# Loading q and k of two batches four heads at a time, in a Nystrom attention with two MLPs

## The chip, the cores and the metric

One core of a Trainium2 chip runs the whole program. The metric is device time in microseconds (us) of one execution. The engines are PE (TensorE, matrix products), DVE (VectorE), ACT (ScalarE), POOL (GpSimd) and SP (SyncE, which here only issues DMAs). "PEld" is the loading of a matmul's stationary operand, which runs beside the matmuls. Data moves on 16 DMA engines that all queues share.

## The reference

Attention with landmarks, then two MLPs on its output. q, k and v have 4 batches, 8 heads, 576 tokens and 64 columns per head.

```
q_lm = q.reshape(B, H, 32, 18, D).mean(axis=3)      # 32 landmarks, each the mean of 18 tokens
k_lm = k.reshape(B, H, 32, 18, D).mean(axis=3)
A  = softmax(scale * q    @ k_lm.T)
Bm = softmax(scale * q_lm @ k_lm.T)
C  = softmax(scale * q_lm @ k.T)
Z  = Bm.T / (norms of Bm); six times: Z = 2*Z - Z @ Bm @ Z
x  = A @ Z @ C @ v                                  # per head, then heads side by side: 2304 x 512
x  = (silu(rms_norm(x) @ w_gate) * (rms_norm(x) @ w_val)) @ w_out      # hidden width 1536
y  = (s * relu(x @ w_in)**2 + b) @ w_out2                              # hidden width 2048
```

The weights come in as 64-bit floats and are narrowed to 32 bits on the core. All large products are made in three passes of halves (a high and a low part of each operand).

## The kernel before

**A planner orders the work.** Each piece of work is handed to a list scheduler with the engines that may do it, an estimated duration and a key (class `Scheduler`, L87). Before anything is issued, it plays the whole program through with its own estimates and so fixes the order of the instructions on every engine. On the chip every engine then works through its own list strictly in order; an instruction that waits holds up all that stand behind it on its engine. Where the planner expects PE to be idle in the first stretch, it puts in matmuls that nobody reads (`warm`, L1245, line 1248 in the profile). What the planner thinks of a load's cost is the number in the load's entry (5.2 for one q or k tile on SP, 9.5 for v).

**Attention** (L401) is done batch by batch. A tile of q or k has 128 partitions: four heads, 32 landmark segments each; a partition holds 18 tokens of 64 columns, 1152 floats. There are two tiles of each, g = 0 and 1, with the heads 2h + g for h = 0 to 3. `load_heads` (L444, DMAs at L446) fills a tile by four DMAs, one head to 32 partitions each. In batch 0 the q tiles are issued on ACT's queue, all others on SP's. v (L457, DMAs at L460) comes in by 18 DMAs of 64 KB per batch. The later batches reuse the same tiles, so their loads wait until the batch before has been read.

Then come the segment sums (`seg_sum`, L471; on DVE at L474 in batch 0, on POOL at L488 to L493 later), their transposes into landmark tiles (L498, L501), the transposes of q and k (`transposed`, L519, PE at L528, copied out by ACT at L532), and the score matmuls, one 32 x 288 block for each head and half (`scores`, L642, L660). In batches 0 and 1 (`fine` false) a score matmul reads the 32 landmark columns of its head and the 32 partitions' columns of its head's transposed tile; in batches 2 and 3 the scores are made with whole tiles in three passes (L648) from a DVE transpose (L537). `c_side` (L669) does C and C @ v, `a_side` (L740) does A and its transpose back; L872 scales A with the norm; `gw` (L810) is the last product of Z, C and v that the first MLP needs.

**The first MLP** runs in units, one for each batch and each 128 columns of the hidden width (12 units a batch): `fused` (L984, PE at L993) folds `gw` into the gate and value weights, `first_mm` (L1009, PE at L1016) multiplies with A, L1032 to L1038 make silu times value, and `out_mm` (L1045, PE at L1061 and L1065) multiplies with w_out. The attention of batch b + 1 runs between the units of batch b.

**Weights** are narrowed by `narrow` (L897): a 512 KB load into one of three `stage` buffers (L904, L906), two ACT instructions (L917, L919), two DVE instructions (L921, L924). The 36 narrowed tiles of the first MLP are stored back (`keptg`, `kepto`) and read again for batches 1 to 3. Below, S1, S2, ... are the stage loads and N1, N2, ... the narrowings, in order; S(n+3) needs the buffer that N(n) has read.

**The second MLP** (L1081, L969: lines 975 and 1091) takes the rest of the run.

**Semaphores of the DMAs.** All DMAs of SP and ACT share eight semaphores in turn (DMAHW0 to 7 in the rows below): a DMA whose semaphore is still in use waits on its engine's list until the eighth DMA before it has landed.

Of the kernel before, what the change touches and what calls it, by code (L numbers as in the profile page):

```python
# [35 lines left out]
SCORE = 0.56  # L36
# [213 lines left out]
def tile_nystrom_attention_two_mlps(  # L250
# [16 lines left out]
    B, H, S, D = q.shape  # L267
    NT, DM = out.shape
    M = 32
    SEG = S // M  # L270
    HB = SEG // 2
    HC = HB * M
# [96 lines left out]
    def consts(_):  # L369
# [12 lines left out]
        out=ident, in_=ones, pattern=[[-1, 128]], compare_op=ALU.is_equal,  # L382
# [18 lines left out]
    def attention(b, t0, t1):  # L401
        first = b == 0
        slow = COLD if first else 1.0
        fine = b >= FINE
# [5 lines left out]
        def at(alts, pos, fn, r=(), w=(), pair=False):  # L410
            mine.append(op(alts, 0.0, fn, r, w, pair or set(alts) == {"dve", "pool"}))
            mine[-1].spare = {"dve": SPA if b else SPA0}
            if not first and "sp" not in mine[-1].alts:
                mine[-1].after = RELB
            at_ops.append(mine[-1])
# [24 lines left out]
        for nm, a in (("k", k), ("q", q)):  # L440
            for g in range(2):
                t = src[nm, g] = Buf(qk_r[nm, g])

                def load_heads(e, t=t, a=a, g=g):  # L444
                    for h in range(4):
                        e.dma_start(  # L446
                            out=t.t[32 * h:32 * h + 32].rearrange("p (t d) -> p t d", d=D),
                            in_=a[b, 2 * h + g].rearrange("(i t) d -> i t d", t=SEG))

                at(("act" if first and nm == "q" else "sp", 2.2 if first and nm == "q" else 5.2),  # L450
                   -0.3 if b else 0, load_heads, w=[t])
        vs = Buf(v_r)

        def vt():
# [5 lines left out]
                e.dma_start(out=vt()[32 * (n % 4):32 * (n % 4) + 32, n // 4], in_=sv[token(b, n)])  # L460

        at(("sp", 9.5), -0.25 if b else 0.01, load_v, w=[vs])

        lmT, bd, tt = {}, {}, {}
        for i, (nm, g) in enumerate((("k", 0), ("k", 1), ("q", 0), ("q", 1))):
# [19 lines left out]
            else:  # L485
# [4 lines left out]
                for n in (4, 2, 1):  # L490
# [3 lines left out]
                    out=lm.t, in0=y()[:, 0], in1=y()[:, 8], op=ALU.add), r=[tmp], w=[lm])  # L494
# [56 lines left out]
        def b_mm(_):  # L551
            for g in range(2):
                if not fine:
                    for h in range(4):
                        p = slice(32 * h, 32 * h + 32)
                        nc.tensor.matmul(
                            out=pB.t[p, 32 * g:32 * g + 32], lhsT=bd["q", g].t[0:D, p],
                            rhs=bd["k", g].t[0:D, p], start=True, stop=True)
                    continue
                for e in range(2):  # L560
                    nc.tensor.matmul(
                        out=pB.t[:, 32 * g:32 * g + 32], lhsT=bdv(bd["q", g])[:, e],
                        rhs=lmT["k", g].t[:, 32 * e:32 * e + 32], start=(e == 0), stop=(e == 1))
# [76 lines left out]
                    else e.tensor_copy(out=zy(1), in_=v2(pY2))), r=[pY2], w=[ZY])  # L640

        def scores(ps, nm, g, hf, p0, r, w):  # L642
            d, t = bd["kq"[nm == "k"], g], tt[nm, g]
            if fine:
                def mm(_):
                    for e in range(2):
# [8 lines left out]
                return  # L655
            def mm(_):
                for h in range(4):
                    p = slice(32 * h, 32 * h + 32)
                    e = slice(D * hf, D * hf + D)
                    nc.tensor.matmul(  # L660
                        out=ps.t[p, 0:HC], lhsT=d.t[e, p],
                        rhs=t.t[e].rearrange("p (t m) -> p t m", m=128)[:, :, p], start=True, stop=True)

            at(("pe", SCORE), p0 + 0.02, mm, r=[d, *[(t, i) for i in range(3)], *r], w=[ps, *w])


        Cv = Buf(cv_r)

        def c_side(g, p0):  # L669
            transposed("k", g, p0)  # L670
            pC = [Buf(ps_r), Buf(ps_r)]
            eC = Buf(eC0_r if first else eC_r)
            cm, cs, rc = Buf(sm_r), Buf(sm_r), Buf(sm_r)
# [65 lines left out]

        def a_side(hf, g, p0):  # L740
            if hf == 0:
                transposed("q", g, p0)
            pA, A, a = Buf(ps_r), Buf(a_ring), Buf(AT_r)
            am, asum = Buf(sm_r), Buf(sm_r)
            AT[hf, g] = a
# [438 lines left out]
    for n in range(len(units) + HALF + 1):  # L1184
        t = T[n]
# [99 lines left out]
```

## Time and profile before

| | us |
|---|---|
| median of three timed runs | 906.83 (901.38 to 908.39) |
| the profiled execution's own time | 903.9 |
| its span, first to last instruction | 902.2 |
| PE busy | 870.2 (96%) |
| DVE busy | 700.9 (78%) |
| ACT busy | 430.0 (48%) |
| mean share of the 16 DMA engines in q1, SP's queue | 38.3% |

The span falls into three stretches. Up to about 61 us the attention of batch 0 runs, and PE is filled up with matmuls of line 1248. From there to about 162 us the first MLP's units of batch 0 run beside the attention of batch 1 and the narrowing of the weights. After that PE works nearly without a gap to the end. PE's busy share therefore says little of the first two stretches: there it counts the filler too.

### The profile page before, as it was taken

The page shows a single profiled execution, that of the slowest core. Times are in us where ns is not written, and L with a number is a line of the kernel's source. Part 1 is how long each engine was busy: PE and PEld are TensorE (multiplying, and loading weights), DVE is VectorE, ACT ScalarE, POOL GpSimd, SP SyncE. Part 2 cuts the span into 40 slices and gives each one's busy share as a digit, 9 for nine tenths or more (in the row PEclk, how much of TensorE's full clock was granted, in tenths as well). Part 3 has the DMA queues.
Part 4 walks back from the last instruction along what each step waited for, and adds up shares of the span by engine and source line. Part 5 has one row for each costly group of instructions (what it writes and reads, how often), then busy time and mean ns, then how long its engine had stood idle before and what let it go on. Part 6 is the DMA issues. An engine that isn't in the chain of part 4 may idle for free.

```text
span 902.2 us, 17055 instructions
## 1 busy us (share of the span) xinstructions
PE 870.2 (96%) x6453; PEld 726.4 (81%) x6453; DVE 700.9 (78%) x1486; ACT 430.0 (48%) x902; POOL 114.4 (13%) x152
## 2 busy tenths in 40 slices
PE   8897899899999999999999999999999999999997
PEld 5576666798788898899888988888888888888896
DVE  5768889889888889799889866676667666666686
ACT  3565566535465345555656533343343334333453
POOL 0442034500465004300000000000000000000000
PEclk9898999999999999999999999999999999999999
DMA  7778998886444432348887200010001000100100
GB/s 162 198 214 283 247 280 236 271 241 216 119 144 141 143 116 84 106 146 272 286 262 252 56 1 1 0 47 1 1 1 47 1 1 1 47 1 1 27 22 24
DMA packets 72899, 105.99 MB, mean 117 GB/s; under 512 B 25968, under 2 KB 46448, under 8 KB 72816
## 3 DMA queue, kind: packets, MB, share of 16 engines
q1 hardware_dynamic: 72240, 103.45, 38.3%
q10 hardware_dynamic: 576, 1.44, 0.7%
q8 instruction: 51, 0.84, 0.4%
q14 instruction: 32, 0.26, 0.1%
HBM read 90.70 MB, written 14.16 MB: 116 GB/s over the span
## 4 chain that ended last, share of the span: by engine, by line
PE 83%; DVE 8%; DMA 5%; ACT 2%; issue 1%; SPq 1%; ACTq 0%; DVEq 0%
PE bank L975 22%; PE bank L1091 22%; PE bank L1016 15%; PE bank L1065 12%; PE bank L1061 3%; PE bank L993 3%; DMA region<-in_q_dram 2%; DVE cmag L921 2%; DMA stage<-in_moe_w_out_dram 2%; PE bank L648 1%; PE bank L828 1%; DMA stage<-in_moe_w_gate_dram 1%; PE bank L1248 1%; DVE wl L893 1%; DVE rawg L924 1%
## 5 line engine op out<-in xcount | busy, mean ns | idle before, releaser
L1016 PE MATMUL bank<-xh,uh 128*128 128x288 f32 x384 | 124.2, 323 | 6.4 <-DVE hbuf L1034 3.1
L975 PE MATMUL bank<-xh,ul 128*128 128x512 f32 (+1 forms) x320 | 117.7, 368 | 0.0
L975 PE MATMUL bank<-xh,uh 128*128 128x512 f32 (+1 forms) x320 | 117.6, 368 | 0.0
L975 PE MATMUL bank<-xl,uh 128*128 128x512 f32 (+1 forms) x320 | 117.6, 368 | 0.0
L1016 PE MATMUL bank<-xl,uh 128*128 128x288 f32 x384 | 114.8, 299 | 0.0
L1016 PE MATMUL bank<-xh,ul 128*128 128x288 f32 x384 | 114.7, 299 | 0.0
L1091 PE MATMUL bank<-wh,hh 128*128 128x512 f32 x288 | 112.4, 390 | 0.3 <-DVE hh L892 0.3
L1091 PE MATMUL bank<-wl,hh 128*128 128x512 f32 x288 | 112.3, 390 | 0.0
L1226 ACT ACTIVATE hbuf<-bank 128x512 f32<-128x512 f32 (+1 forms) x79 | 43.9, 556 | 143.4 <-PE bank L975 143.3
L1091 PE MATMUL bank<-wh,hl 128*128 128x512 f32 x288 | 112.0, 389 | 0.0
L1016 PEld LDWEIGHTS bank<-xh,uh 128*128 128x128 f32 x384 | 73.6, 192 | 27.3 <-issue 5.0
L1065 PE MATMUL bank<-hh,wh 128*128 128x288 f32 x288 | 87.9, 305 | 1.1 <-ACT xbuf L1075 1.1
L1065 PE MATMUL bank<-hl,wh 128*128 128x288 f32 x288 | 84.9, 295 | 0.1
L1065 PE MATMUL bank<-hh,wl 128*128 128x288 f32 x288 | 84.6, 294 | 0.0
L893 DVE TENSOR_TENSOR hl<-hbuf,hh 128x512 fp32r<-128x512 f32 (+2 forms) x123 | 73.1, 595 | 2.3
L1016 PEld LDWEIGHTS bank<-xl,uh 128*128 128x128 f32 x384 | 73.7, 192 | 0.5
L1016 PEld LDWEIGHTS bank<-xh,ul 128*128 128x128 f32 x384 | 73.7, 192 | 0.0
L975 PEld LDWEIGHTS bank<-xh,uh 128*128 128x128 f32 x320 | 60.2, 188 | 11.1
L975 PEld LDWEIGHTS bank<-xl,uh 128*128 128x128 f32 x320 | 60.0, 188 | 10.9
L975 PEld LDWEIGHTS bank<-xh,ul 128*128 128x128 f32 x320 | 60.1, 188 | 10.2
L917 ACT ACTIVATE ca<-stage 128x512 f32<-128x512 f32 x68 | 45.9, 675 | 42.6 <-DMA stage<-in_moe_w_out_dram 12.0
L892 DVE CAST uh<-region 128x512 fp32r<-128x512 f32 x56 | 23.9, 426 | 54.4 <-PE bank L975 54.4
(193 smaller groups left out, 1822.9 us busy)
## 6 DMA issues: line engine op xcount, KB each, us to landing
rawo<-kepto SPq DMA_DIRECT2D x84, 256.0 KB, 3.3
rawg<-keptg SPq DMA_DIRECT2D x36, 512.0 KB, 3.9
stage<-in_moe_w_out_dram SPq DMA_DIRECT2D x28, 512.0 KB, 5.2
stage<-in_moe_w_in_dram SPq DMA_DIRECT2D x16, 512.0 KB, 4.6
stage<-in_moe_w_gate_dram SPq DMA_DIRECT2D x12, 512.0 KB, 5.3
stage<-in_moe_w_val_dram SPq DMA_DIRECT2D x12, 512.0 KB, 5.5
keptg<-rawg SPq DMA_DIRECT2D x12, 512.0 KB, 6.3
region<-in_k_dram SPq DMA_DIRECT2D x32, 144.0 KB, 5.3
```

Of the source, the lines that this page charges most:

```text
L648: nc.tensor.matmul(out=ps.t[:, 0:HC], lhsT=part(u, "bd")[:, 128 * e:128 * e + 128], rhs=part(y, "t").rearrange("p (t e i) -> p t e i", e=2 ...
L892: else e.tensor_copy(out=hi(), in_=src())), r=r, w=[wh], pair=True)
L893: b = op({"dve": t_dve(n), "pool": t_pool(n)}, key, lambda e: e.tensor_tensor(out=lo(), in0=src(), in1=hi().bitcast(F32), op=ALU.subtract) ...
L917: op(("act", 0.08 + t_act(512)), key, lambda e: e.activation(out=a.t, in_=word(1).bitcast(F32), func=ACTF.Copy, scale=2.0 ** -112), r=[st, ...
L921: op(("dve", t_dve(512)), key, lambda e: e.scalar_tensor_tensor(out=m.t, in0=word(1), scalar=-2 ** 31, in1=m.t, op0=ALU.bitwise_and, op1=A ...
L975: nc.tensor.matmul(out=ps.t[:, 0:n], lhsT=w[a].t[:, ks], rhs=x[y].t[:, kd, 0:n], start=(kd == 0 and i == 0), stop=(kd == KD - 1 and i == 2))
L993: nc.tensor.matmul(out=pU[g].t[m, 0:256], lhsT=gw[b].t[p, m], rhs=r.t[p, :, 128 * k:128 * k + 128], start=True, stop=True)
L1016: nc.tensor.matmul(out=ps.t[:, 0:HC], lhsT=u[a].t[:, 256 * g + 128 * part:256 * g + 128 * part + 128], rhs=x[y].t.rearrange("p k n -> p (k ...
L1061: nc.tensor.matmul(out=A[c].t[:, 0:HC], lhsT=r.t[:, 128 * c:128 * c + 128], rhs=h.t, start=(f == 0), stop=(f == F1 - 1))
L1065: nc.tensor.matmul(out=A[c].t[:, 0:HC], lhsT=w[a].t[:, 128 * c:128 * c + 128], rhs=hs[y].t[:, 0:HC], start=(f == 0 and i == 0), stop=(f == ...
L1091: nc.tensor.matmul(out=A[c].t, lhsT=hs[a].t[:, s], rhs=w[y].t, start=(f == 0 and i == 0), stop=(f == F2 - 1 and i == 2))
L1226: e.activation(out=r.t[:, 0:n], in_=ps.t[:, 0:n], func=ACTF.Relu) if e is nc.scalar
```

## The change

Batches 0 and 1 load each q and k tile with a single DMA of four heads to 128 partitions; the tile then holds the heads 4i to 4i + 3 in order, not the heads of one parity. The sums, landmarks and transposes are the same per tile. The matmuls that combine heads (`b_mm`, `scores`) look up in which tile and which partitions head 2h + g now lies (`loaded`) and write where they wrote before. Since a group g now reads both tiles, `c_side(0)` transposes both k tiles, and `a_side` of g = 0 both q tiles. Batches 2 and 3 keep the four DMAs a tile. q of batch 0 is issued on SP's queue, and the planner's cost for a tile of batches 0 and 1 is 3.64 in place of 5.2 (and 2.2 for q on ACT). With other costs, the planner also orders other things anew.

```diff
                 def load_heads(e, t=t, a=a, g=g):
+                    if not fine:
+                        e.dma_start(
+                            out=t.t.rearrange("p (t d) -> p t d", d=D),
+                            in_=a[b, 4 * g:4 * g + 4].rearrange("h (i t) d -> (h i) t d", t=SEG))
+                        return
                     for h in range(4):
                         e.dma_start(
                             out=t.t[32 * h:32 * h + 32].rearrange("p (t d) -> p t d", d=D),
                             in_=a[b, 2 * h + g].rearrange("(i t) d -> i t d", t=SEG))
 
-                at(("act" if first and nm == "q" else "sp", 2.2 if first and nm == "q" else 5.2),
-                   -0.3 if b else 0, load_heads, w=[t])
+                at(("sp", 5.2 if fine else 3.64), -0.3 if b else 0, load_heads, w=[t])
...
+        def loaded(g, h):
+
+            n = 2 * h + g
+            return n // 4, slice(32 * (n % 4), 32 * (n % 4) + 32)
...
             def mm(_):
                 for h in range(4):
-                    p = slice(32 * h, 32 * h + 32)
+                    i, p = loaded(g, h)
                     e = slice(D * hf, D * hf + D)
                     nc.tensor.matmul(
-                        out=ps.t[p, 0:HC], lhsT=d.t[e, p],
-                        rhs=t.t[e].rearrange("p (t m) -> p t m", m=128)[:, :, p], start=True, stop=True)
-
-            at(("pe", SCORE), p0 + 0.02, mm, r=[d, *[(t, i) for i in range(3)], *r], w=[ps, *w])
+                        out=ps.t[32 * h:32 * h + 32, 0:HC], lhsT=bd[other, i].t[e, p],
+                        rhs=tt[nm, i].t[e].rearrange("p (t m) -> p t m", m=128)[:, :, p], start=True, stop=True)
+
+            at(("pe", SCORE), p0 + 0.02, mm, r=[*[bd[other, j] for j in range(2)],
+                *[(tt[nm, j], i) for j in range(2) for i in range(3)], *r], w=[ps, *w])
...
         def c_side(g, p0):
-            transposed("k", g, p0)
+            for j in (g,) if fine else (0, 1) if g == 0 else ():
+                transposed("k", j, p0)
...
             if hf == 0:
-                transposed("q", g, p0)
+                for j in (g,) if fine else (0, 1) if g == 0 else ():
+                    transposed("q", j, p0)
```

SP's list at its start, before, with the semaphores that each DMA waits for (`region` holds the q, k and v tiles):

```order
L446 DMA region<-in_k_dram 32x1152 x4
L446 DMA region<-in_k_dram 32x1152 [waits DMAHW1_49]
L446 DMA region<-in_k_dram 32x1152 [waits DMAHW3_49]
L446 DMA region<-in_k_dram 32x1152 [waits DMAHW5_49]
L446 DMA region<-in_k_dram 32x1152 [waits DMAHW7_49]
L460 DMA region<-in_v_dram 32x8x64 [waits DMAHW0_49]
L460 DMA region<-in_v_dram 32x8x64 [waits DMAHW1_49]
```

And now:

```order
L446 DMA region<-in_k_dram 128x1152 x2
L446 DMA region<-in_q_dram 128x1152 x2
L464 DMA region<-in_v_dram 32x8x64 x4
L464 DMA region<-in_v_dram 32x8x64 [waits DMAHW0_49]
L464 DMA region<-in_v_dram 32x8x64 [waits DMAHW1_49]
L464 DMA region<-in_v_dram 32x8x64 [waits DMAHW2_49]
L464 DMA region<-in_v_dram 32x8x64 [waits DMAHW3_49]
L464 DMA region<-in_v_dram 32x8x64 [waits DMAHW4_49]
```

Four DMAs stand where sixteen stood (eight of them on ACT's list). The fifth to eighth of v now wait for the four of k and q, and the ninth for the first of v.

SP's list around the loads of batch 1, before (the first row closes the small loads after S1 to S3; the `stage` rows are S4, S5, S6 and S7):

```order
L388 DMA b_sb<-in_moe_b_dram 128x1
L446 DMA region<-in_k_dram 32x1152 x8
L446 DMA region<-in_q_dram 32x1152 x8
L906 DMA stage_91<-in_moe_w_val_dram 128x4x128
L906 DMA stage_92<-in_moe_w_gate_dram 128x4x128
L906 DMA stage_93<-in_moe_w_val_dram 128x4x128
L937 DMA keptg_114<-rawg_85 128x1024
L460 DMA region<-in_v_dram 32x8x64 x18
L906 DMA stage_91<-in_moe_w_gate_dram 128x4x128
```

And now:

```order
L388 DMA b_sb<-in_moe_b_dram 128x1
L446 DMA region<-in_k_dram 128x1152 x2
L446 DMA region<-in_q_dram 128x1152 x2
L464 DMA region<-in_v_dram 32x8x64 x18
L919 DMA stage_91<-in_moe_w_val_dram 128x4x128
L919 DMA stage_92<-in_moe_w_gate_dram 128x4x128
L919 DMA stage_93<-in_moe_w_val_dram 128x4x128
L950 DMA keptg_114<-rawg_85 128x1024
L451 DMA region<-in_k_dram 32x1152 x4
L919 DMA stage_91<-in_moe_w_gate_dram 128x4x128
```

The 18 loads of v for batch 1 have moved from between S6 and S7 to ahead of S4. Four loads of k for batch 2 now stand ahead of S7.

SP's list around the loads of q and v for batch 2, before (the `stage` rows are S29 to S33):

```order
L906 DMA stage_92<-in_moe_w_val_dram 128x4x128
L446 DMA region<-in_q_dram 32x1152 x4
L904 DMA stage_93<-in_moe_w_out_dram 128x512
L949 DMA kepto_129<-rawo_90 128x512
L446 DMA region<-in_q_dram 32x1152 x4
L904 DMA stage_91<-in_moe_w_out_dram 128x512
L460 DMA region<-in_v_dram 32x8x64 x18
L906 DMA stage_92<-in_moe_w_gate_dram 128x4x128
L906 DMA stage_93<-in_moe_w_val_dram 128x4x128
```

And now:

```order
L919 DMA stage_92<-in_moe_w_val_dram 128x4x128
L451 DMA region<-in_q_dram 32x1152 x8
L917 DMA stage_93<-in_moe_w_out_dram 128x512
L962 DMA kepto_129<-rawo_90 128x512
L464 DMA region<-in_v_dram 32x8x64 x18
L917 DMA stage_91<-in_moe_w_out_dram 128x512
L919 DMA stage_92<-in_moe_w_gate_dram 128x4x128
L919 DMA stage_93<-in_moe_w_val_dram 128x4x128
```

S31 stood ahead of the 18 loads of v and now stands behind them; all eight loads of q stand ahead of S30.

The rest of the lists is ordered much as before. DVE has the same instructions ahead of the last two L872 of batch 1, but for two or three. PE has 121 filler matmuls in place of 161, the same matmuls otherwise, and in batch 1 the 18 transposes of q stand together between the ninth and the tenth group of L993, where nine of them stood between the eighth and the ninth. Ahead of the first two L866 of batch 0 (which broadcast the norm for L872) there were 35 and then 15 fillers on PE's list, and now there are none.

## Rows read from the trace of the kernel before

**Rows 1.** Windows: us; each engine's busy us (instructions); PE clock, DMA share, GB/s.

```profile
56.00:66.00 10.00, 9.99 (x91) 8.57 (x89) 4.98 (x13) 5.37 (x11) 6.49 (x10) 1.00 0.76 222
...
120.00:140.00 20.00, 19.07 (x282) 13.41 (x281) 18.39 (x51) 12.10 (x30) 10.27 (x14) 1.00 0.91 272
...
160.00:200.00 40.00, 39.00 (x312) 34.47 (x313) 34.36 (x72) 16.23 (x38) 12.63 (x17) 0.96 0.85 253
...
500.00:600.00 100.00, 100.00 (x472) 84.32 (x472) 72.73 (x132) 40.21 (x70) 0.00 (x0) 1.00 0.07 17
```

**Rows 2.** Chain that ended last, first 62 us: by line; two pieces (start, us).

```profile
by line: DMA region<-in_q_dram 19.2%; PE bank L1248 12.4%; SPq L460 9.6%; DMA stage<-in_moe_w_gate_dram 7.2%; PE bank L848 6.8%; issue 5.4%; DVE cmag L921 3.6%; PE bank L828 3.6%; PE bank L726 2.5%; DVE region L762 2.3%; ACTq L446 2.1%; DVE
...
8.89 5.23 DMA region<-in_q_dram
...
20.64 4.49 DMA stage<-in_moe_w_gate_dram
```

**Rows 3.** Timeline of the start: start us, us, engine, line; idle time before, its releaser.

```profile
0.80 8.41 ACTq L446 DMA_DIRECT2D region<-in_q_dram  x8
0.80 8.12 SPq L446 DMA_DIRECT2D region<-in_k_dram  x8
...
8.71 2.12 DVE L474 TENSOR_REDUCE region<-region 128x64 f32<-128x1152 f32 x1 [7.13 <-DMA region<-in_k_dram]
...
10.09 10.51 SPq L460 DMA_DIRECT2D region<-in_v_dram  x18
...
13.62 6.30 DVE L474 TENSOR_REDUCE region<-region 128x64 f32<-128x1152 f32 x3 [2.78 <-DMA region<-in_k_dram]
...
25.15 0.66 ACT L917 ACTIVATE ca<-stage 128x512 f32<-128x512 f32 x1 [2.57 <-DMA stage<-in_moe_w_gate_dram]
```

**Rows 4.** Windows of 2 us in the start, columns as in rows 1.

```profile
0.00:2.00 2.00, 0.88 (x5) 0.64 (x6) 0.53 (x17) 0.00 (x0) 0.50 (x5) 1.00 0.24 28
...
4.00:6.00 2.00, 2.00 (x13) 1.36 (x11) 0.00 (x0) 0.00 (x0) 0.00 (x0) 1.00 1.01 214
6.00:8.00 2.00, 0.11 (x2) 0.00 (x0) 0.00 (x0) 0.00 (x0) 0.00 (x0) 1.00 1.00 205
...
24.00:26.00 2.00, 0.33 (x16) 0.22 (x16) 1.83 (x11) 0.85 (x2) 0.00 (x0) 0.98 1.08 373
```

**Rows 5.** The page's DMA issues: count, KB each, median us to landing.

```profile
rawg<-keptg SPq DMA_DIRECT2D x36, 512.0 KB, 3.9
...
region<-in_k_dram SPq DMA_DIRECT2D x32, 144.0 KB, 5.3
```

**Rows 6.** Timeline of SP's queue around v of batches 1 and 2.

```profile
47.64 11.07 SPq L460 DMA_DIRECT2D region<-in_v_dram  x18
58.81 0.40 SPq L906 DMA_DIRECT2D stage<-in_moe_w_gate_dram  x1
...
127.26 1.85 SPq L446 DMA_DIRECT2D region<-in_q_dram  x4
...
135.94 0.35 SPq L904 DMA_DIRECT2D stage<-in_moe_w_out_dram  x1
136.39 11.83 SPq L460 DMA_DIRECT2D region<-in_v_dram  x18
```

**Rows 7.** Timeline of PE and DVE between 52 and 66 us.

```profile
52.84 4.16 PE L1248 MATMUL bank<-ones 128*128 128x256 bf16 x35
...
62.70 0.46 DVE L1034 SCALAR_TENSOR_TENSOR hbuf<-hbuf,bank 128x288 f32<-128x288 f32 x1 [2.23 <-ACT hbuf L1032]
...
65.89 1.22 DVE L921 SCALAR_TENSOR_TENSOR cmag<-stage,cmag 128x512 int32<-128x512 int32 x1
```

**Rows 8.** Timeline of DVE and PE towards the end of batch 1's attention.

```profile
116.96 0.66 PE L993 MATMUL bank<-rawg,gw 64*32 64x256 f32 x16
...
134.69 0.66 PE L993 MATMUL bank<-rawg,gw 64*32 64x256 f32 x16
...
146.05 0.69 DVE L921 SCALAR_TENSOR_TENSOR cmag<-stage,cmag 128x512 int32<-128x512 int32 x1
...
161.65 0.66 PE L993 MATMUL bank<-rawg,gw 64*32 64x256 f32 x16
```

More of the change, by code (lines that the diff above doesn't have):

```diff
@@ L554, in b_mm @@
                     for h in range(4):
-                        p = slice(32 * h, 32 * h + 32)
+                        i, p = loaded(g, h)
                         nc.tensor.matmul(
-                            out=pB.t[p, 32 * g:32 * g + 32], lhsT=bd["q", g].t[0:D, p],
-                            rhs=bd["k", g].t[0:D, p], start=True, stop=True)
+                            out=pB.t[32 * h:32 * h + 32, 32 * g:32 * g + 32], lhsT=bd["q", i].t[0:D, p],
+                            rhs=bd["k", i].t[0:D, p], start=True, stop=True)
                     continue
@@ L642, in scores @@
         def scores(ps, nm, g, hf, p0, r, w):
-            d, t = bd["kq"[nm == "k"], g], tt[nm, g]
+            other = "kq"[nm == "k"]
             if fine:
@@ L657, in mm @@
                 for h in range(4):
-                    p = slice(32 * h, 32 * h + 32)
+                    i, p = loaded(g, h)
                     e = slice(D * hf, D * hf + D)
                     nc.tensor.matmul(
-                        out=ps.t[p, 0:HC], lhsT=d.t[e, p],
-                        rhs=t.t[e].rearrange("p (t m) -> p t m", m=128)[:, :, p], start=True, stop=True)
-            at(("pe", SCORE), p0 + 0.02, mm, r=[d, *[(t, i) for i in range(3)], *r], w=[ps, *w])
+                        out=ps.t[32 * h:32 * h + 32, 0:HC], lhsT=bd[other, i].t[e, p],
+                        rhs=tt[nm, i].t[e].rearrange("p (t m) -> p t m", m=128)[:, :, p], start=True, stop=True)
+            at(("pe", SCORE), p0 + 0.02, mm, r=[*[bd[other, j] for j in range(2)],
+                *[(tt[nm, j], i) for j in range(2) for i in range(3)], *r], w=[ps, *w])
         Cv = Buf(cv_r)
         def c_side(g, p0):
-            transposed("k", g, p0)
+            for j in (g,) if fine else (0, 1) if g == 0 else ():
+                transposed("k", j, p0)
             pC = [Buf(ps_r), Buf(ps_r)]
```

## The prediction

> **What bounds the kernel now.** I read the windows first. From 160 us on PE is busy 39.0 of 40 us, later 100 of 100 [rows 1]: that stretch is PE's, the change takes no product out of it, and it will last as long as now, wherever it starts. So the question is how much earlier it starts. Between 120 and 140 us DVE is busy 18.4 of 20 us [rows 1]; it does batch 1's attention, the narrowing and the units' work, and its list sets the pace from about 66 us on. Between 56 and 66 us it is busy only 4.98 of 10 us [rows 1]: there it waits. The chain of the first 62 us [rows 2] names, as its largest part, the loads of q (19.2%), and then the issuing of v (9.6%) and the first stage load (7.2%). The timeline of the start [rows 3] says how: DVE's first segment sum starts at 8.71 us, when the first k tile has landed; it idles 2.78 us more for the second, and the last three sums end at 13.62 + 6.30 = 19.92. ACT idles 2.57 us until 25.15 for the first stage load, with the attention's work behind that instruction on its list.
>
> Why the loads take so long shows in the short windows [rows 4]. With all 16 DMA engines busy (share 1.00 and 1.01) they move 205 and 214 GB/s into tiles of 32 partitions; between 24 and 26 us, mostly stage loads to 128 partitions, 373 GB/s at a share of 1.08. The page agrees: 512 KB to 128 partitions land in 3.9 us, 144 KB to 32 partitions in 5.3 [rows 5].
>
> **The change, part by part.**
>
> *The first sums.* Batch 0's 16 loads are 16 x 144 KiB = 2.36 MB. The first 2 us move 28 GB/s, 56 KB [rows 4], so data flows from about 1.75 us; at 215 GB/s 2.36 MB take 11.0 us, to 12.75. The last load lands at 8.89 + 5.23 = 14.12 [rows 2], 1.4 us behind its last byte. At 373 GB/s a tile of 590 KB takes 1.6 us, and k comes first, no longer mixed with q: the tiles land at 1.75 + 1.6 + 1.4 = 4.75, then 6.3, 7.9 and 9.5 us. Four sums of 2.1 us (6.30/3) from 4.75 run without a gap to 13.15, against 19.92: **6.8 us** earlier. The lower bound is the old rate: tiles at 5.9, 8.6, 11.4 and 14.1 us, sums done at 16.2, 3.7 us earlier, since k still goes ahead of q. I take 373, because its row is the nearest to 128-partition loads with full engines.
>
> [...]
>
> *The stage loads.* SP issues v's 18 loads from 10.09 to 20.60 [rows 3], the later ones 0.49 us apart, because each waits for the eighth DMA before it. Now the fifth to eighth wait for the k and q tiles and the ninth for the first v load, behind the last q tile, about 10.0 us; ten more follow at 0.49 us, so S1 goes out at about 14.9 instead of 20.64, 5.7 us earlier. With the old rate it is 1.1. This does not add to the first term: the chain needs both. But ACT's wait of 2.57 us shrinks, as its list now has the softmax of C ahead of the first stage tile: 0 to 2.6, I take **1.0**.
>
> *The hole at 56 to 66 us.* S7 is issued at 58.81, after v of batch 1 has held SP for 11.07 us [rows 6], and N7 starts on DVE at 65.89 [rows 7]. Ahead of it DVE also waits for PE, where 35 fillers of 4.16 us in all stand before the L866 that DVE needs, and then 2.23 us for the first hidden tile [rows 7]. Now v stands ahead of S4, in time in which SP waits for a free stage buffer anyhow, and those fillers are gone. S7 needs N4, and k of batch 2 is ahead of it, so the hole does not close for certain. DVE's idle time there is 10 - 4.98 = 5.0 us: between 0 and 5.0, I take **3.0**.
>
> *S31.* It was issued at 135.94, just ahead of the 11.83 us of v for batch 2 [rows 6]; now it follows them. Its N31 runs at 146.05 [rows 8]. With a lead of 9 us over the old times SP reaches q at 118, and eight loads of 0.46 us (1.85/4), S30 and v take it to about 134.5. S31 then lands 4.5 us later (4.49 for the first stage load [rows 2]), and after 1.3 us of ACT N31 could start at 140.3, where DVE would be ready at 137. Some of these 3.3 us fill with other work that DVE has before N31: 0 to 3.3 lost, I take **2.5**.
>
> *At nothing:* the eight issues on ACT, which has nothing else before 9 us; the 40 fillers, which are not waited for where PE is the bound; batch 1's own faster loads, long landed before its work is due; the score matmuls, which are as many and as large as before.
>
> Sum: 6.8 + 1.0 + 3.0 - 2.5 = **8.3 us**. The profiled execution took 903.9 us, which gives 895.6. The median of the timed runs lies 2.9 above that execution; on it the sum gives 898.5. The mean of all four executions is 905.1, which gives 896.8: I say **897**.
>
> **The rivals.**
>
> *The transfer is no faster.* The DMA engines are already full at 205 GB/s [rows 4]; if they and not the target limit the rate, four DMAs in one save only waits. [...] Against it stand the 373 GB/s at the same share. The sums gain 3.7, S1 gains 1.1, and since the chain needs both, some 2 to 3 remain, and the hole gives 1: 901 to 902.
>
> *The lead is used up.* From 66 to 162 us DVE's list could be paced by something that does not move with the start: the three stage buffers, or the DMA engines, at a share of 0.91 [rows 1]. Then the units catch up with the old times: 903 to 905. Against it, both start earlier too, and the faster loads of two batches relieve the engines.
>
> *More.* The hole closes, S31 costs nothing, ACT's wait goes: 7.0 + 2.6 + 5.0 = 14.6, 889 to 892.
>
> *Slower: batch 1's q comes a unit late.* Its transposes need both transposed-tile buffers, which both groups of k now hold until all scores of C are made; so all 18 stand behind the ninth L993, where nine stood ahead of it. From the ninth L993, at 116.96, to the tenth are 17.7 us [rows 8]. If the work on A falls back by one such stretch, less the third of it that already lay there, some 12 us, the twelfth L993, at 161.65 us [rows 8], with which PE's own stretch begins, loses 12 and gains 8.3: 903.9 + 3.7 = 907.6, and with the smaller gain of the first rival 913. It decides from a delay of 8.3 us on. Against it, the scores of C on PE's list have moved forward in exchange.
>
> **How the numbers follow.** Chances: the forecast (a gain of 5 to 11 us) 0.50, no faster transfer 0.17, lead used up 0.12, more 0.15, slower 0.06. The runs shown lie up to 0.6% from their median, so about 1% is what can be told from no change. 1% is 9 us, and the forecast's own range lies about that line: half of it, most of "more" and a little of the rest count as faster, 0.45; slower by over 1% takes the last rival nearly whole, 0.05; the rest, 0.50, is within. The range is 889 to 905: the lower end is "more", the upper takes in the first two rivals; left out are the slower case and half of what lies at the ends, under 0.2.
>
> **What would show it.** Right: the first L474 near 4.8 us and the last ending near 13.2; windows above 330 GB/s before 10 us; S1 near 15 and S7 near 48 to 50 us; N7 before 58; the twelfth L993 near 153 us; from there an unchanged stretch. Wrong: about 215 GB/s in the first 10 us (first rival); N7 early but the twelfth L993 near 161 (second); more than 20 us from the ninth L993 to the tenth (slower). What would make it wrong without these is a new stall on PE's or DVE's list after 160 us, where DVE works 34.4 of 40 us [rows 1] and has little room.

## The result, and the profile after

The changed kernel takes **893.49 us** (median of four runs, 892.03 to 895.56) against 905.4 (four runs of the kernel before): ratio **0.9869, 95% interval 0.9838 to 0.9899**. Timed a second time, beside other kernels, it took 896.31 (six runs), ratio 0.9896 (0.9872 to 0.9921). Over all ten runs the median is 895.2, some 10 us less than before. The forecast was 897.0, range 889 to 905. The rows below are of the profiled run of 892.31 us, span 890.7.

The start, on DVE (start us, us, engine, line, operation; in brackets the idle time before and its releaser) and in windows of 2 us (columns as in rows 1):

```profile
4.47 8.32 DVE L484 TENSOR_REDUCE region<-region 128x64 f32<-128x1152 f32 x4 [2.89 <-DMA region<-in_k_dram]
```

```profile
2.00:4.00 2.00, 2.00 (x11) 1.40 (x10) 0.00 (x0) 0.08 (x1) 0.00 (x0) 1.00 0.98 325
4.00:6.00 2.00, 2.00 (x14) 1.61 (x12) 1.53 (x1) 0.53 (x2) 0.00 (x0) 1.00 1.00 396
6.00:8.00 2.00, 1.43 (x14) 1.16 (x14) 2.00 (x2) 1.39 (x4) 0.00 (x0) 1.00 1.03 405
```

L484 is the old L474. The sums no longer wait for single tiles: four in one piece, done at 12.79 where rows 3 have 19.92. At the same share of the DMA engines, 1.00, the loads now move 396 GB/s where they moved 214 [rows 4].

SP's queue up to the seventh stage load (S1 at 15.79, S4 at 37.79, S7 at 52.45), and the first stage tile's ACT instruction:

```profile
1.73 0.91 SPq L446 DMA_DIRECT2D region<-in_q_dram  x2
2.68 13.06 SPq L464 DMA_DIRECT2D region<-in_v_dram  x18
15.79 0.45 SPq L919 DMA_DIRECT2D stage<-in_moe_w_gate_dram  x1
...
20.39 1.48 SPq L446 DMA_DIRECT2D region<-in_q_dram  x2
27.74 9.94 SPq L464 DMA_DIRECT2D region<-in_v_dram  x18
37.79 0.39 SPq L919 DMA_DIRECT2D stage<-in_moe_w_val_dram  x1
...
50.62 1.73 SPq L451 DMA_DIRECT2D region<-in_k_dram  x4
52.45 0.38 SPq L919 DMA_DIRECT2D stage<-in_moe_w_gate_dram  x1
```

```profile
20.03 0.67 ACT L930 ACTIVATE ca<-stage 128x512 f32<-128x512 f32 x1 [0.37 <-DMA stage<-in_moe_w_gate_dram]
```

S1 is 4.85 us earlier than in rows 2, and ACT's wait for it fell from 2.57 us [rows 3] to 0.37. v of batch 1 is issued at 27.74 instead of 47.64 [rows 6], ahead of S4. S7 comes 6.4 us earlier than in rows 6, behind the k loads of batch 2, before which SP stands from 40.72 to 50.62.

On DVE, N6 and N7, and later N31 and N32; then the last two pairs of L885 (before: L872), by which attention ends:

```profile
55.73 0.68 DVE L934 SCALAR_TENSOR_TENSOR cmag<-stage,cmag 128x512 int32<-128x512 int32 x1
59.99 0.74 DVE L934 SCALAR_TENSOR_TENSOR cmag<-stage,cmag 128x512 int32<-128x512 int32 x1
...
141.60 0.69 DVE L934 SCALAR_TENSOR_TENSOR cmag<-stage,cmag 128x512 int32<-128x512 int32 x1 [1.70 <-ACT cmag L932]
143.73 0.69 DVE L934 SCALAR_TENSOR_TENSOR cmag<-stage,cmag 128x512 int32<-128x512 int32 x1
...
149.91 0.81 DVE L885 TENSOR_TENSOR region<-region,bank 128x288 f32<-128x288 f32 x2
151.63 0.82 DVE L885 TENSOR_TENSOR region<-region,bank 128x288 f32<-128x288 f32 x2
```

The same pairs in the kernel before:

```profile
160.04 0.81 DVE L872 TENSOR_TENSOR region<-region,bank 128x288 f32<-128x288 f32 x2
161.76 0.82 DVE L872 TENSOR_TENSOR region<-region,bank 128x288 f32<-128x288 f32 x2
```

N7 leads by 5.9 us [rows 7], the pair that starts at 149.91 by 10.1. From that pair to the end of the span are 740.8 us, before 902.2 - 160.04 = 742.2. So 10.1 of the 11.5 us between the two profiled spans are made ahead of that pair, and PE's stretch behind it is nearly what it was, 1.4 us shorter. The start of that pair is the yardstick below; it is called the last pair but one.

### The profile page after: what moved, and what is told of

It is laid out like the page before. It is cut to its first block, busy times and chain, and to the rows that moved or that the text cites. A ratio compares the mean times of both kernels' runs of the same rounds, so it can differ in the third digit from the quotient of the medians.

```text
span 890.7 us, 16937 instructions
## 1 busy us (share of the span) xinstructions
PE 861.8 (97%) x6413; PEld 719.7 (81%) x6413; DVE 695.9 (78%) x1491; ACT 431.8 (48%) x899; POOL 114.1 (13%) x150
## 4 chain that ended last, share of the span: by engine, by line
PE 78%; DVE 10%; DMA 6%; ACT 3%; issue 2%; SPq 0%; DVEq 0%; ACTq 0%
PE bank L988 22%; PE bank L1104 22%; PE bank L1029 12%; PE bank L1078 11%; DMA stage<-in_moe_w_in_dram 2%; PE bank L1006 2%; DVE cmag L934 2%; DMA stage<-in_moe_w_out_dram 1%; PE bank L1261 1%; PE bank L658 1%; PE bank L1074 1%; PE bank L841 1%; PE bank L596 1%; DMA region<-in_q_dram 1%; DMA stage<-in_moe_w_val_dram 1%
## 5 line engine op out<-in xcount | busy, mean ns | idle before, releaser
L988 PEld LDWEIGHTS bank<-xh,ul 128*128 128x128 f32 x320 | 60.1, 188 | 10.1
```

The source lines that it names most:

```text
L988: nc.tensor.matmul(out=ps.t[:, 0:n], lhsT=w[a].t[:, ks], rhs=x[y].t[:, kd, 0:n], start=(kd == 0 and i == 0), stop=(kd == KD - 1 and i == 2))
```

## The experiments

All ratios are to the kernel before, timed on the same chip. Behind the interval stand moments of the profiled run (us), which lies up to 5 us from its kernel's median (single heads 903.45, batch 1 alone 895.18); line numbers shift by a few.

| kernel | median | ratio, 95% interval | sums end | S4 | S7 | N7 | last pair but one |
|---|---|---|---|---|---|---|---|
| before | 905.4 | | 19.92 | 41.39 | 58.81 | 65.89 | 160.04 |
| changed | 893.49 | 0.9869 (0.9838 to 0.9899) | 12.79 | 37.79 | 52.45 | 59.99 | 149.91 |
| changed, again | 896.31 | 0.9896 (0.9872 to 0.9921) | 13.02 | 39.19 | 55.27 | 62.89 | 153.05 |
| single heads, new order | 900.51 | 0.9948 (0.9931 to 0.9966) | 15.47 | 46.05 | 59.71 | 68.03 | 159.79 |
| 64 partitions | 902.53 | 0.9963 (0.9944 to 0.9982) | 15.94 | 44.70 | 60.66 | 68.71 | 160.96 |
| 128 partitions, short rows | 898.79 | 0.9927 (0.9908 to 0.9947) | 14.07 | 43.58 | 56.53 | 64.81 | 155.08 |
| merged in batch 0 only | 896.81 | 0.9907 (0.9886 to 0.9927) | 13.02 | 42.74 | 55.75 | 63.71 | 155.19 |
| merged in batch 1 only | 899.97 | 0.9940 (0.9917 to 0.9963) | 15.58 | 42.92 | 55.21 | 62.74 | 152.88 |
| before, q on SP | 903.85 | 0.9992 (0.9972 to 1.0012) | 15.31 | 37.77 | 55.28 | 63.92 | 159.88 |
| merged, old costs | 906.31 | 1.0001 (0.9986 to 1.0015) | 16.39 | 35.59 | 52.98 | 65.82 | 164.10 |
| batch 2's k held back | 903.7 | 0.9977 (0.9953 to 1.0002) | 13.05 | 39.60 | 51.59 | 60.44 | 158.96 |

The first theory (A) was the prediction's: wider loads end the sums earlier, and that lead reaches the end. Its main rival (B) is the order: the planner makes its lists from the costs of the loads, and the change altered these too (3.64 for 5.2, and q of batch 0 on SP).

### The form of the load, at the changed kernel's order

The next five kernels keep the changed kernel's instructions on PE, DVE, ACT and POOL in its order; only the DMAs of k and q differ. First, single heads:

```diff
-                        e.dma_start(
-                            out=t.t.rearrange("p (t d) -> p t d", d=D),
-                            in_=a[b, 4 * g:4 * g + 4].rearrange("h (i t) d -> (h i) t d", t=SEG))
+                        for h in range(4):
+                            e.dma_start(
+                                out=t.t[32 * h:32 * h + 32].rearrange("p (t d) -> p t d", d=D),
+                                in_=a[b, 4 * g + h].rearrange("(i t) d -> i t d", t=SEG))
```

> The changed kernel with its tile layout and its order on every engine, but each k and q tile of batches 0 and 1 loaded as before in four DMAs of 32 partitions, one head each; all sixteen of a batch are now on SP. Theory A (the gain is the width of the loads: a DMA over 128 partitions moves 400 GB/s, where several over 32 partitions move 215): the four tiles of batch 0, 590 KB each, land one after the other at 215 GB/s, 2.7 us apart, so the sums of L484 begin near 5 and end near 15.5 us (12.79 in the changed kernel, 19.92 before); SP issues sixteen instead of four, v stands behind them and the stage loads come at 20 us or later; time 897 to 904. Theory B (the gain is the new order, which the planner made of a load cost of 3.64 for 5.2 and of q on SP): the order is kept, so the time stays within 2 us of the changed kernel, 891.5 to 895.5, even if the first sums are late.

Measured: 900.51 us. The windows and the sums:

```profile
4.00:6.00 2.00, 1.14 (x9) 0.76 (x8) 0.46 (x1) 0.00 (x0) 0.00 (x0) 1.00 1.00 224
6.00:8.00 2.00, 0.99 (x9) 0.76 (x9) 1.68 (x1) 1.25 (x3) 0.00 (x0) 0.94 1.06 237
```

```profile
5.54 2.14 DVE L485 TENSOR_REDUCE region<-region 128x64 f32<-128x1152 f32 x1 [3.96 <-DMA region<-in_k_dram]
8.11 2.12 DVE L485 TENSOR_REDUCE region<-region 128x64 f32<-128x1152 f32 x1 [0.43 <-DMA region<-in_k_dram]
...
13.31 2.16 DVE L485 TENSOR_REDUCE region<-region 128x64 f32<-128x1152 f32 x1 [0.46 <-DMA region<-in_q_dram]
```

The rate is the old one, a tile lands every 2.6 us, and the sums end at 15.47. Some half of the gain goes, as A has it. But 5 us of gain remain (0.0052 x 905 = 4.7) without one wider load. B in its pure form has fallen (it wanted 895.5 or less). A's number holds, and the 4.45 us by which the sums still lead could be its reason for the rest; the run with q on SP, below, says otherwise.

Two heads a DMA, 64 partitions (these lines stand in place of the merged load):

```diff
+                        for i in range(2):
+                            e.dma_start(
+                                out=t.t[64 * i:64 * i + 64].rearrange("p (t d) -> p t d", d=D),
+                                in_=a[b, 4 * g + 2 * i:4 * g + 2 * i + 2].rearrange("h (i t) d -> (h i) t d", t=SEG))
```

> The changed kernel, order kept, each k and q tile of batches 0 and 1 in two DMAs of two heads, over partitions 0 to 63 and 64 to 127: rows of 4608 bytes as in the merged and the single-head loads, eight issues a batch instead of four or sixteen. Theory A (rate by the partitions that a DMA covers): if 64 neighbouring partitions are no faster than 32, 215 to 240 GB/s from 4 to 8 us, first sum of L484 at 5.0 to 5.6, sums end near 15.5 us as with single heads (15.47), time 896 to 901. Theory C (the number of DMAs): 300 to 400 GB/s, sums end at 12.8 to 13.8 us and the time is 893 to 896.

Measured: 902.53 us, its windows and first sum:

```profile
4.00:6.00 2.00, 0.93 (x5) 0.31 (x3) 0.00 (x0) 0.00 (x0) 0.00 (x0) 1.00 1.05 233
6.00:8.00 2.00, 1.95 (x9) 1.78 (x9) 1.99 (x1) 0.89 (x2) 0.00 (x0) 1.00 0.99 224
```

```profile
6.01 2.14 DVE L485 TENSOR_REDUCE region<-region 128x64 f32<-128x1152 f32 x1 [4.43 <-DMA region<-in_k_dram]
```

Half as many DMAs as with single heads, and the rate is the same, 224 to 233 GB/s. So theory C, the count, has fallen. With rows of 4608 bytes and full engines, DMAs over 32 and over 64 partitions move 224 to 237 GB/s in these runs, and those over 128 move 396 to 405 in the changed kernel and 417 to 422 under the old costs, below. (The bytes of one DMA rise too, 144, 288 and 576 KiB; the first doubling changed nothing.) The time came out a little above A's range and is not told apart from the single heads'.

All 128 partitions, but a quarter of the tokens a DMA:

```diff
+                        for t0, t1 in ((0, 5), (5, 10), (10, 14), (14, 18)):
+                            e.dma_start(
+                                out=t.t.rearrange("p (t d) -> p t d", d=D)[:, t0:t1],
+                                in_=a[b, 4 * g:4 * g + 4].rearrange("h (i t) d -> (h i) t d", t=SEG)[:, t0:t1])
```

> The changed kernel, order and layout kept, each k and q tile of batches 0 and 1 again in four DMAs, but every one over all 128 partitions (tokens 0 to 5, 5 to 10, 10 to 14 and 14 to 18 of each segment). As many DMAs on SP as with single heads, at the same 144 KB; only the partitions differ. Theory A (width of the load): over 330 GB/s from 2 to 8 us and first sum of L484 near 5 us; sums end near 13 to 14 us, time 893 to 897. Theory C (the number of DMAs on SP, sixteen issues of about half a microsecond and the semaphores that they share): as with single heads, sums end past 15 us, the stage loads at 20 us or later, time 897 to 904 and within 1.5 us of the single-head kernel.

Measured: 898.79 us, above A's range and inside C's, but 1.7 us from the single heads, where C wanted 1.5 at most; the sums end at 14.07, just past A's 14 and before C's 15.

```profile
4.00:6.00 2.00, 1.62 (x14) 1.28 (x12) 0.76 (x1) 1.00 (x3) 0.00 (x0) 1.00 0.91 253
6.00:8.00 2.00, 0.60 (x6) 0.43 (x7) 1.68 (x2) 0.37 (x2) 0.00 (x0) 1.00 0.89 266
```

253 to 266 GB/s, at shares of 0.91 and 0.89: neither case. The edit also cut the rows from 4608 bytes (18 x 64 x 4) to 1024 or 1280, and the bytes of one DMA from 576 KiB to between 128 and 160. The share is the smaller part of the difference: 253 / 0.91 = 278 GB/s, an estimate for full engines from the first window, where rows of 4608 bytes reach 396. So the experiment is not clean. It suggests a second condition beside the 128 partitions, in the rows or in the bytes of a DMA; no run changed either alone.

### Which batch

In both edits the batch that is left out gets the single-head loads of the first experiment (not shown again).

```diff
-                    if not fine:
+                    if first:
...
```

> Merged loads in batch 0 only; batch 1's k and q by single heads in the changed kernel's layout; order kept. Theory A with the gain at the start: the sums end at 12.8 us as in the changed kernel, batch 1's loads have cover, time 892 to 895.5. Rival D (batch 1's loads carry a part: its k sums and the stage loads behind them on SP come sooner): stage loads S4 to S6 later than 37.8 to 38.8 us by 3 or more, time 896 to 900.

```diff
-                    if not fine:
+                    if not fine and not first:
...
```

> Merged loads in batch 1 only; batch 0's k and q by single heads in the changed kernel's layout; order kept. Theory A with the gain at the start: as with single heads everywhere, sums end near 15.5 us, stage loads at 20 us or later, time within 1.5 us of that kernel, 897 to 904. Rival D (batch 1's loads carry a part): 2 us or more below the kernel with single heads everywhere.

The changed kernel once more, beside the three kernels that follow:

> The changed kernel itself, unedited, timed beside the next three on one chip, as the yardstick for differences below one per cent. Every theory: 892 to 895.5. What it must decide is whether merged loads in batch 0 alone (896.81 earlier) are really slower than merged loads in both: if batch 1's loads carry a part, this stays 2 us or more below 896.8; if they carry none, it comes out at 895.5 or more.

Measured: 896.81 with batch 0 alone merged, 899.97 with batch 1 alone, 893.49 and 896.31 with both. Batch 0 carries most of it (900.51 to 896.81). Of batch 1 the medians decide nothing: against the second timing of the changed kernel it is worth 0.5 us, against the first 3.3. By the sentences above, batch 0 alone speaks for rival D (its time, and S4 5.0 us later); batch 1 alone, 0.5 us below the single heads, and the repeat at 896.31 speak against it. The profiled runs do show a place. With batch 1's k and q by single heads, v and S4 stand behind sixteen issues, S4 goes out at 42.74, and ACT waits for it; next to it the same 19 fillers on PE, here and in the changed kernel:

```profile
47.27 0.66 ACT L936 ACTIVATE ca<-stage 128x512 f32<-128x512 f32 x1 [2.12 <-DMA stage<-in_moe_w_val_dram]
...
49.35 4.17 PE L1267 MATMUL bank<-ones 128*128 128x256 bf16 x19 [1.78 <-ACT region L517]
```

```profile
47.99 2.23 PE L1261 MATMUL bank<-ones 128*128 128x256 bf16 x19 [0.70 <-ACT region L511]
```

```profile
46.00:48.00 2.00, 1.57 (x8) 0.93 (x8) 1.82 (x5) 0.73 (x2) 0.58 (x1) 0.50 1.03 293
48.00:50.00 2.00, 0.65 (x4) 0.45 (x4) 1.55 (x3) 2.00 (x6) 1.12 (x2) 0.50 0.99 330
50.00:52.00 2.00, 2.00 (x11) 1.40 (x10) 1.53 (x3) 1.98 (x3) 2.00 (x2) 0.50 0.43 170
```

The windows are of the kernel with batch 0 alone merged: PE idles 1.78 us behind ACT, its granted clock is 0.50 from 46 to 52 us, and the fillers, which stand on PE's list like any matmul, take 4.17 us; in the changed kernel, where the clock is 1.00 from 48 to 52 us, they take 2.23. N6 comes 3.3 us later. That is where batch 1's loads show in this pair of runs.

The repeat is of use by itself: the same program lies 2.5 us apart in its two profiled runs, and the difference is there by N4 (48.34 and 51.08). So one pair of traces does not tell 2 us of the first 60 from chance.

### The queue and the order

The kernel before, its own order on every engine, with q of batch 0 issued on SP behind k instead of on ACT:

```diff
...
-                    for h in range(4):
+                    if first and nm == "q":
+                        held_q.append((t, a, g))
+                        return
+                    for t, a, g in [(t, a, g)] + held_q * (first and g == 1):
+                        for h in range(4):
...
```

> The kernel before, its head order, its single-head loads and its order on every engine kept; only the eight q loads of batch 0 go from ACT's queue to SP's, behind the eight of k. Theory E (half of the gain at the start is the one queue: tiles land one after the other instead of all four together, so DVE's sums run beside the loads): first L474-sum near 5.5 us, the four end near 15.5 instead of 19.92, stage loads near 19.5 to 20.6; time 900 to 903.5. Theory A in its pure form (only the wide loads gain): the sums end within 1 us of before or their gain does not reach the end, time 904 to 907.

Measured: 903.85 us, ratio 0.9992: no gain that can be told from none. Yet the sums begin and end as theory E says:

```profile
5.49 2.15 DVE L479 TENSOR_REDUCE region<-region 128x64 f32<-128x1152 f32 x1 [3.91 <-DMA region<-in_k_dram]
...
13.14 2.17 DVE L479 TENSOR_REDUCE region<-region 128x64 f32<-128x1152 f32 x1 [0.44 <-DMA region<-in_q_dram]
...
63.92 1.22 DVE L926 SCALAR_TENSOR_TENSOR cmag<-stage,cmag 128x512 int32<-128x512 int32 x1
...
112.10 0.45 DVE L1039 SCALAR_TENSOR_TENSOR hbuf<-hbuf,bank 128x288 f32<-128x288 f32 x1 [1.62 <-ACT hbuf L1037]
```

A lead of 4.6 us at 15.31 is 2.0 at N7 and 0.2 at the last pair but one. At 112 us, after a window (105 to 110) at a granted clock of 0.50, DVE waits 1.62 us that it does not wait before the change. An earlier start is not yet an earlier end.

The other way round, merged loads under an order made from the old cost lines:

```diff
-                at(("sp", 5.2 if fine else 3.64), -0.3 if b else 0, load_heads, w=[t])
+                at(("act" if first and nm == "q" else "sp", 2.2 if first and nm == "q" else 5.2),
+                   -0.3 if b else 0, load_heads, w=[t])
```

> The changed kernel's merged loads, head sorting and joint transposes, but planned with the old cost lines: q of batch 0 on ACT at 2.2, all other k and q loads on SP at 5.2. The planner makes another order from it. So far the loads' width at the new order was worth about 5 us (single heads 900.5, merged 893.5 and 896.3) and the new order at single heads about 4 (the kernel before with q on SP 903.9, single heads in the new order 900.5). Theory H (the two add up, so width alone carries over to another order): sums end at 13 to 15 us and the time is 897 to 901. Theory I (the lead of the sums lives only in the new order, the old one eats it as it ate the 4.6 us of the queue): sums just as early, time 902 to 906.

Measured: 906.31 us, ratio 1.0001: theory I, 0.3 us above its range. The loads are fast here (417 to 422 GB/s from 4 to 8 us), the sums end 3.5 us earlier than before the change (and 3.6 later than in the changed kernel, with q on ACT's queue), S7 comes at 52.98, as in the changed kernel. But v of batch 1 is back behind S6, as in the kernel before, and the end of attention has another place on the lists:

```profile
43.13 9.75 SPq L465 DMA_DIRECT2D region<-in_v_dram  x18
52.98 0.40 SPq L920 DMA_DIRECT2D stage<-in_moe_w_gate_dram  x1
```

```profile
62.30 0.45 DVE L1048 SCALAR_TENSOR_TENSOR hbuf<-hbuf,bank 128x288 f32<-128x288 f32 x1 [4.43 <-ACT hbuf L1046]
...
65.82 0.69 DVE L935 SCALAR_TENSOR_TENSOR cmag<-stage,cmag 128x512 int32<-128x512 int32 x1
...
164.10 0.81 DVE L886 TENSOR_TENSOR region<-region,bank 128x288 f32<-128x288 f32 x2
173.06 0.82 DVE L886 TENSOR_TENSOR region<-region,bank 128x288 f32<-128x288 f32 x2 [0.21 <-PE bank L880]
```

N7 is where it was before the change, and the last pair comes at 173.06, 11.3 us later than before, after a wait of only 0.21 us: nothing holds it up there, the lists place it late. The lists differ here from those of the kernel before as well as from the new ones. So neither this order nor the width gives the result alone: single heads in the new order 0.9948, merged loads in the old-cost order 1.0001, both 0.9869 and 0.9896.

### The hole at 42 to 60 us

The changed kernel with one line more, which the planner takes as an earliest time for batch 2's k loads:

```diff
+                if b == 2 and nm == "k":
+                    mine[-1].after = 62.0
```

> The changed kernel with batch 2's k loads held back in the plan to 62 us, so that on SP they stand behind S7 and not ahead of it (in the changed kernel SP waits 9.8 us for PE's transposes of batch 1's k before them, and S7 is issued at 52.45). The planner makes a new order from about 45 us on. Theory F (the hole at 42 to 60 us is S7 behind these loads): S7 near 49.5 to 50.5, right after the fourth narrowing frees its buffer, N7 at 57 or earlier, time 889 to 892. Rival G (the hole is PE and ACT of batch 1's attention, S7 has slack): N6 still past 55, N7 past 59, time 892 to 896.

Measured: 903.7 us, worse than both theories. S7 goes out at 51.59, only 0.9 us earlier, because N4, which must free its buffer, now begins at 50.83 and not at 48.34. So the run hardly moves S7 and cannot decide between F and G. The trace of the changed kernel can. The second of N7's two ACT instructions, and what stands just ahead of N7 on DVE's list:

```profile
57.36 0.68 ACT L932 ACTIVATE cmag<-stage 128x512 int32<-128x512 uint8 x1
```

```profile
59.62 0.46 DVE L1047 SCALAR_TENSOR_TENSOR hbuf<-hbuf,bank 128x288 f32<-128x288 f32 x1 [0.89 <-ACT hbuf L1045]
```

ACT was done for N7 at 58.04. N7 starts at 59.99 because its place on the list is behind the third hidden tile, for which DVE waited 0.89 us. So S7 has slack there, as rival G has it. What the run with the loads held back loses comes later: from N7 to the last pair but one are 98.5 us, in the changed kernel 89.9 and, repeated, 90.2. The planner had made another order from 45 us on, and its difference of 8 us is as large as the whole gain under study.

### The clock

Fillers laid into planned idle time up to 125 us instead of 60, in three kernels (the changed one, the one before with q on SP, and the one before):

```diff
-WARM1 = 60.0
+WARM1 = 125.0
```

> The changed kernel with its filler matmuls (L1261) laid into planned idle time of TensorE up to 125 us instead of 60: 41 more fillers, nothing else moves. Theory J (half-clock stretches after idle time of TensorE eat part of the lead after 60 us and make the runs spread): fewer windows at a granted clock of 0.5 between 60 and 120 us, 12th L1006 below 152, time 890 to 894. Rival K (the loads and DVE set that stretch; the clock costs nothing there, or the fillers stand in the way of real matmuls): 894 to 899.

> The kernel before with q of batch 0 on SP (sums at 15.3, but 903.85 and the lead gone by 117 us, after a window at half clock from 105 to 110) and with fillers up to 125 us. Theory J: with the clock held the lead of 2 to 4 us at the fourth narrowing reaches the end, 899 to 902 and 2 us or more below the kernel before with the same fillers. Rival K: the lead goes all the same, 902 to 906 and within 1.5 us of the kernel before with the same fillers.

> The kernel before with fillers up to 125 us instead of 60, as the yardstick for the run with q on SP and the same fillers. Theory J: 901 to 904, a little below the kernel before. Rival K: 904 to 908.

Measured: 898.96, 904.1 and 906.19 us; ratios 0.9923 (0.9900 to 0.9946), 0.9989 (0.9974 to 1.0005) and 1.0012 (0.9997 to 1.0028). None of the times that theory J forecast has come: the changed kernel is no faster for 41 more fillers, by the ratios 2 to 5 us slower. Nor did they raise its clock: of the windows of 20 us between 60 and 120 us one has a granted clock of 0.91 with them (60 to 80) and without (80 to 100), the other two 1.00. Between the last two kernels lie 2.1 us; that just meets J's 2, but the intervals hold the 1.4 of the kernels without these fillers as well, and neither comes near the 4.6 of the sums. With q on SP the clock was higher with the fillers: all such windows from 80 to 160 us have 1.00, where without them it was 0.82 from 100 to 105 us and 0.50 from 105 to 110, and the time is 904.1 all the same. So the half-clock window of that kernel may be a part of its wait; it is not what kept the lead from the end.

## Why the prediction was right

**Right in the first term.** The sums' 6.8 us came out as 7.1 (6.9 in the repeat), from tiles at the rate that I took from the nearest row, 373 GB/s; the measured rate is 396 to 405. The lower bound at the old rate, 16.2 us for the end of the sums and k ahead of q, was measured twice: 15.47 and 15.31. The 7.0 us that "More" sets for this term is shown by no row and no run: at 373 GB/s the term is 6.8, and the runs showed 7.1 and 6.9.

**Right in the second, low in size.** ACT's wait shrank by 2.2 us where I took 1.0. S1 came at 15.79 and not at 14.9: v's 18 issues took 13.06 us, a little over the sum of waits that I had counted.

**The hole failed as a step.** I forecast S7 at 48 to 50, N7 before 58 and a gain of 3.0. S7 came at 52.45, N7 at 59.99, and the lead, 7.6 us at N1 (32.42 against 39.98), fell to 5.9 at N7. What I had not read: the k loads of batch 2 ahead of S7 wait for PE's transposes of batch 1's k, 9.9 us on SP's list. Nor was S7 what N7 waited for: N7 stands behind hidden tiles on DVE's list, and those waited for PE and ACT. Why PE and ACT are late there was not tested.

**S31 came late as forecast, and its price did not last.** It went out at 136.00, its N31 waited 1.70 us and its lead fell to 4.5 us. The next one, N32, had 11.2 again: the loss fills with other work.

**From N7 on, a gain of another kind.** The lead grew from 5.9 to 10.1 us at the last pair but one, and the forecast has no term for that. DVE's own account tells what it is: an instruction starts after all the time that DVE was busy ahead of it and all the time that it idled. Two stretches, up to N7 and from N7 to the last pair but one (columns as in rows 1), before and now:

```profile
0.00:65.89 65.89, 57.33 (x674) 42.30 (x675) 41.40 (x117) 33.17 (x81) 19.14 (x31) 0.90 0.77 192
65.89:160.04 94.15, 81.60 (x827) 59.09 (x826) 83.55 (x191) 58.79 (x130) 25.84 (x33) 0.96 0.88 262
```

```profile
0.00:59.99 59.99, 51.07 (x648) 37.82 (x656) 41.66 (x120) 34.04 (x80) 25.15 (x38) 0.94 0.73 220
59.99:149.91 89.92, 79.11 (x819) 56.92 (x814) 78.35 (x190) 58.02 (x129) 17.29 (x25) 0.98 0.87 268
```

Up to N7 DVE is about as busy as before and idles 6.2 us less. From there on it idles 1.0 us more, but with nearly the same instructions it is busy 5.2 us less. Of the 10.1 us, then, 5.2 are idle time, which is what my sum of 8.3 was made of, and 4.9 are busy time, for which it has nothing. That the sum came out near 10 is luck to that extent.

The busy time is that of the narrowings. L921, now L934, from N7 on (ns: shortest, median, longest; first and last start):

```profile
L921 DVE SCALAR_TENSOR_TENSOR cmag<-stage,cmag x27: 630/685/1724, 65.9 to 157.9; 128x512 int32<-128x512 int32 x27
```

```profile
L934 DVE SCALAR_TENSOR_TENSOR cmag<-stage,cmag x27: 674/685/836, 60.0 to 148.4; 128x512 int32<-128x512 int32 x27
```

The medians are equal, the longest are not. Counted one by one, the 66 DVE instructions of `narrow` ahead of the last pair but one took 52.7 us before and take 47.8 now; 14 of them lasted over 0.75 us before, 8 do now. All of these long ones ran beside an instruction of POOL for three tenths of their time or more, and none that ran while POOL was idle took over 0.70 us. POOL's segment sums of batch 1, for example, ended at 73.7 us before, 7.8 behind the start of N7; now they end at 60.9, 0.9 behind it. So the new order seems to gain its 5 us because fewer narrowings meet POOL's work. That is read from traces; no run moved POOL's work alone.

It goes with the order and not with the loads. From N7 to the last pair but one DVE is busy 77.9 to 78.4 us in the seven traces of the new order (the second to the eighth row of the table), 83.4 with q on SP and 81.4 under the old costs. What the loads move is DVE's idle time up to N7: 18.3 and 21.0 us with merged loads in both batches, 25.8 with single heads, whose profiled run, though, is 3 us slower than its median and shows nothing of its gain. With q on SP the idle time up to N7 falls by 2.2 us, and 1.9 of it come back behind N7.

**Batch 1's loads at nothing** was not settled: 0.5 to 3.3 us, with a visible place in one trace.

**The premise that was missing.** I took a lead at 13 us as a lead at 160. In two orders it is not: 4.6 us were worth 1.4 with q on SP, 3.5 were worth nothing under the old costs. "The lead is used up" got 0.12, and it holds in both. In the changed kernel it holds in part: 7.1 us at the sums are 5.2 us of idle time at the last pair but one, and the rest of the lead there seems due to the lists that the planner made from the new costs, which I read only where they touch SP's queue. The sum of 8.3 against some 10 is right in size, with the hole too high by about 5 us (3.0 gained forecast, 1.7 lost from N1 to N7) and nothing set down for DVE's shorter narrowings. "The transfer is no faster" was false by 396 GB/s, but its time, 901 to 902, is nearly that of single heads in the new order, 900.5. "Batch 1's q a unit late" was false: from the ninth L1006 (the old L993) to the tenth are 15.6 us, before 17.7 [rows 8], and the twelfth comes at 151.52, where I had said 153.

## What to carry to other kernels

Here a load that fills 128 partitions with rows of 4608 bytes moved 1.7 to 1.8 times what loads of 32 or 64 partitions moved (396 to 405 GB/s against 224 to 237) with the same engines full; look for it where a profile shows a DMA share of 1.00 and little over half the GB/s of other loads in the same run, as here 205 and 214 beside 373 [rows 4]. Do not carry a lead over 150 us of listed work without looking for the wait that would eat it: follow one landmark near the end of the stretch through both traces, and take the engine's busy time ahead of it apart from its idle time: here each was half of the gain, and only one of them had been forecast. Where a planner makes the lists, a change of a cost is a change of the order, and here such changes were worth as much as the change itself; test the two apart.

## What was not expected

- The same program's profiled runs lie 2.5 us apart, and the repeat has a granted clock of 0.50 in the three windows from 42 to 48 us, where the first run has 0.68, 0.50 and 0.97. The last of them in the repeat:

```profile
46.00:48.00 2.00, 2.00 (x21) 0.85 (x19) 0.50 (x2) 0.95 (x3) 1.53 (x2) 0.50 0.90 341
```

  PE was busy through the two windows before it in both runs (2.00 of 2.00 us); why the clock rises 2 us later in the repeat stays open.
- 128 partitions with rows of 1024 and 1280 bytes reach 253 to 266 GB/s from 4 to 8 us, hardly more than 32 partitions with rows of 4608 (224 to 237).
- 41 fillers in PE's planned idle time made the changed kernel 2 to 5 us slower: its last pair but one starts at 157.27, and without them at 149.91 and 153.05.
